# Six tiles in turn for the gathered rows of the routed experts, and each gather issued behind the turn that frees its tile

## The chip, the cores and the metric

The kernel runs on one core of a Trainium2 chip. The metric is the device time of one execution in microseconds; for the kernel before it is 903.7 us, the median of 3 runs from 902.4 to 906.5. Inputs and outputs lie in the chip's DRAM, tiles that engines work on lie in SBUF, and matrix products are written to PSUM.

## The reference, cut to what matters

Three layers follow each other, all in float32:

```python
# 1. delta-rule attention, 4 x 8 heads, 768 tokens, head_dim 48  -> x [3072, 384]
# 2. routed mixture: 8 experts, each token goes to the one with the largest logit
logits = x @ w_gate
e_idx  = np.argmax(logits, axis=1)
for e in range(8):
    mask = e_idx == e
    h  = np.maximum(x[mask] @ w1[e], 0.0)          # 384 -> 1024
    ye = h @ w2[e]                                 # 1024 -> 384
    out[mask] = gate_w[mask, None] * eom[mask, e, None] * ye
# 3. a dense mixture over all 3072 rows
h = np.maximum(np.maximum(x @ w1, x @ w2), x @ w3) # 384 -> 768, float64 weights
y = (h @ w_out)                                    # 768 -> 384
```

What counts here is layer 2: the rows of one expert lie scattered over x, so each expert's rows have to be gathered before they can be multiplied.

## The kernel before, in words

**Stages.** The attention with the routing of its rows fills about the first third of the time, the routed experts the second, the dense mixture the last. The order of the work on each engine is written out by hand: a unit (a small function) is given a time as a fraction of its run, the units of a run are sorted by that fraction, and each engine then executes its own instructions strictly in that order. A fraction therefore sets only the order; when an instruction starts is decided by its engine and by semaphores.

**Runs.** The routed experts are worked off in ten runs (`Moe.run`, line 1106). Runs 0 to 3 have 256 rows each, in two chunks of 128; runs 4 to 9 have 440, 416, 404, 388, 380 and 368 rows, in four chunks of 110, 104, 101, 97, 95 and 92 (`CAPS`, line 656). The weights of a run have a key: runs 4 to 9 have the keys 2 to 7.

**A run's steps.** `ids` (line 834) loads the entries of a run's list. `gather` (line 850) brings one chunk's rows, 1536 bytes each, from the DRAM tensor xd into a tile xg, with an indirect DMA that GpSimd (POOL) issues. `xpose` (line 863) turns a block of 128 features of all chunks of a run on TensorE, ScalarE makes the hi part and VectorE the lo part (xh, xl); a run has three such turns. `m1` (line 889) is the first product, eight units of nine matmuls, after which ScalarE and VectorE make hh and hl; `o1` (line 904) is the second product, three units of 24 matmuls, copied out by ScalarE into y.

**Where the turns lie.** In runs 2 to 8 the order on TensorE is: eight m1, turn 0 of the next run, o1 number 0, turn 1, o1 number 1, turn 2, o1 number 2. So turn 0 of run k + 1 stands between the two products of run k, and it needs all chunks of run k + 1.

**The gathers before the change.** There are four tiles xg, taken in turn over all chunks. The gathers of run 4 are issued, in POOL's order, at the start of run 3, and those of run k + 1 at the start of run k for k from 3 to 8 (line 1141); those of run 3 at the start of run 1, those of run 2 near the end of run 0 (line 1131).

**What else stands in the queues.** POOL also makes the lo part of the second weight of the next run, four instructions `w_..l` (`split`, line 700, and line 1145), placed from 0.5 of the run on, each behind ScalarE's hi part. The queue of SyncE (SP) loads the raw weights: the first weight (line 1147) at 0.6 and the second (line 1149) at 0.15 of a run, each into one tile that the split of the weight before must have read. It also moves 24 pieces of the dense mixture's weights (`Decode.units`, line 611), which VectorE and ScalarE work on between the units of the runs (line 1155), four pieces per run in runs 4 to 8.

**Memory.** The tiles xg are in the pool gp. The pool named moe (line 679) is opened after the attention's pools have been closed; the results y (line 910) lie in it, two tiles of 3 x 480 floats per partition.

Of the kernel before, what the change touches and what calls it, by code (L numbers as in the profile page):

```python
# [8 lines left out]
F32 = mybir.dt.float32  # L9
# [9 lines left out]
LIST = 3200          # entries of an expert's list  # L19
COLS = 3584          # of the first mixture's result  # L20


def merge(*lists):
    """Interleaves lists of units evenly."""
    items = []
    for li, l in enumerate(lists):
        n = len(l)
        for j, f in enumerate(l):
            items.append(((j + 0.5) / n, li, j, f))
    items.sort(key=lambda t: t[:3])  # L30
    return [t[3] for t in items]


class Attn:
    """Delta-rule attention in chunks of 32 tokens, and the routing of its rows.

    With k raw, n = |k| + 1e-6 and w = b / n^2 of a chunk's rows:
      U = (I + diag(w) tril(K K', -1))^-1 diag(w) (diag(n) V - K S)
      Y = Q S + tril(Q K', -1) U,  S <- S + K' U
    A sequence's eight heads are (j, b), j of 2, b of 4; g is the sequence: pairs (j = 0, 1) for each b, g.  # L40
    Partitions of the tiles of k, v and u: (b, 32 tokens); of y: (g, 32 tokens). "h" below is (g, j).
    """

    def __init__(s, ctx, tc, psum, big, hp, gp, kqt, knv, bt, wgt, xd, tab, ctab, cum, ident, wrm, x2):
# [4 lines left out]
        s.NI = 24          # chunks  # L49
        s.NP = 12          # pairs of chunks  # L50
        s.NSL = 6          # slabs of four chunks
# [7 lines left out]
        s.NA = 24          # units of stage A before the chain  # L59
# [6 lines left out]
        # slabs; steps of the chain: for the loads and scales, start and end of the inverses  # L66
        # of the vector engine, microseconds for the inverses in the steps of the chain
# [14 lines left out]
    def consts(s):  # L82
# [6 lines left out]
        # -beta of the blocks' tokens: partition (chunk of the slab, h, b), free (slab, k)  # L89
# [11 lines left out]
        # lists without tokens; an entry: row of xd, factor, token  # L101
# [9 lines left out]
        # routing  # L111
# [29 lines left out]
    # ---- stage A: the products of a chunk's tokens  # L141
    def loadKQ(s, i):
        """K' | Q' of a chunk: partition (head of a pair, d), free (b, pair of heads, k | q, t)"""
# [48 lines left out]
    # ---- stage B: inverses of four chunks; partition (chunk, h, b), free (i, k)  # L192
# [6 lines left out]
    def inv_n1(s, sl):  # L199
        """|k|^2 from the diagonals, then the strict triangles alone"""  # L200
# [7 lines left out]
    def inv_n2(s, sl):  # L208
        """n^2 = |k|^2 + 2e-6 |k| + 1e-12"""
# [12 lines left out]
    def inv_n3(s, sl):  # L222
        """-w, and n with one step of Newton for 1 / |k|"""
# [13 lines left out]
    def inv_step(s, ms):  # L237
        """Step m of one slab, in two parts, or of two slabs, [(slab, m)]: each hides the other's latency"""
# [37 lines left out]
    def steps(s, starts):  # L276
        """[(slabs that begin, time, unit, slabs that end)] of the inverses of slabs, {slab: first index}"""
# [12 lines left out]
    # ---- stage C: the chain over the chunks  # L290
    def load32(s, i):
        """Rows of k and v: partition (b, t), free (h, d)"""
        if i >= s.NI:
            return
        s.kv[i] = s.p2.tile([128, 2, 8, 48], F32, tag="kv", name=f"kv{i}", bufs=3)
        s.nc.sync.dma_start(s.kv[i], s.knv[i])
# [92 lines left out]
    # ---- stage R: routing of four chunks' rows  # L389
# [10 lines left out]
    def r_l(s, q):  # L400
        """The two gates' products of four chunks' rows: partition (chunk, gate and expert)"""
# [71 lines left out]
    def r_s(s, us):  # L473
        """A routing's rows go into the lists."""
# [5 lines left out]
    def warm(s, n):  # L480
        """Keeps the tensor engine's clock up over a wait."""
# [6 lines left out]
    # ---- the schedule  # L488
    def run(s, pre, tail):
# [15 lines left out]
        # the scales of slabs 1 and 2 as well  # L505
# [18 lines left out]
        # units of the inverses and of stage A over the steps; step -1 is before the chain  # L524
# [68 lines left out]
class Decode:  # L593
    """float64 weights, given as their 64 bits, to float32r parts: w = hi + lo, in DRAM.

    hi has a weight's sign, exponent and first 11 bits after the point; lo the rest, rounded to 12 bits.
    Weights under float32's normal range become 0.
    """

    N = 384          # doubles of a piece, per partition  # L600
# [10 lines left out]
    def units(s, raw, w):  # L611
        """Units of the next piece; raw: a function that gives its [128, 2 N] int32; w: [128, 4 N] int32"""
# [23 lines left out]
class Run:  # L636
    """A part of an expert's list: n entries in chunks of ct, its weights' key, the tags of their tiles."""
# [7 lines left out]
class Moe:  # L645
    """Both mixtures over rows that the routing has put into lists, one list per expert.

    Experts 0 and 1 come in two parts each: the first has tokens of the first 16 chunks, while the
    routing goes on. The others come in the order of their counts. The results follow each other
    without gaps as columns of x2, their tokens and factors in ctab.  # L650
    Float32 products: each operand is split exactly into two float32r parts, hi + lo; a product is
    hi hi + hi lo + lo hi.
    """
# [4 lines left out]
    def __init__(s, tc, cp, big, hp, gp, xd, x2, tab, ctab, w1, w2, dec, out):  # L658
# [5 lines left out]
        s.nh = 0  # L664
        nc, G = s.nc, s.nc.gpsimd
        # row: counts, limits, 8 zeros, starts, experts 2 to 7 of the runs, first parts' counts, experts 0 and 1, excess
# [14 lines left out]
    # ---- weights  # L681
# [585 lines left out]
```

## Time and profile before

| | |
|---|---|
| time, median of 3 runs (range) | 903.7 us (902.4 to 906.5) |
| span of the profiled execution, first to last instruction | 901.6 us |
| mean granted TensorE clock, share of full | 0.958 |
| TensorE matmul busy | 793.7 us, 88% of the span |
| VectorE busy | 478.3 us, 53% |
| ScalarE busy | 318.0 us, 35% |
| GpSimd busy | 251.0 us, 28% |
| gathers of routed rows | 32 |

The profiled execution has no time of its own beside its span; the span is 2.1 us under the median of the runs. PE is TensorE, DVE is VectorE, ACT is ScalarE, POOL is GpSimd, SP is SyncE, and SPq is SyncE's instruction queue, which issues DMAs. L868 is line 868 of the kernel. A timeline row reads: start and duration in us, engine, line, operation, output tile <- input tiles, shape, count, and in brackets how long the engine had been idle before and what ended that. A busy share is an average over stages with different limits, so it is read stage by stage.

### The profile page before, as it was taken

To read this page: it belongs to the slowest core of one execution; us is meant where nothing else is said; L and a number is where in the kernel's file an instruction comes from. 1 tells how busy PE (TensorE), PEld (TensorE's weight loads), DVE (VectorE), ACT (ScalarE), POOL (GpSimd) and SP (SyncE) were. 2 spreads that over 40 slices of the span, in tenths; PEclk is the share of its full clock that TensorE was granted. 3 is DMA by queue.
4 is the path that set the end of the run, shared out by engine and by line. 5 is a ranking of instruction groups with operands and counts; after the bars stand their busy time and mean duration, and the time that the engine had idled before them with its cause. 6 is when DMAs were issued, how large, how long until landed. Compare 5 with 4: busy or idle time off the path is not lost. (4 is left out here: it accounts for less than half of the span.)

```text
span 901.6 us, 20554 instructions
## 1 busy us (share of the span) xinstructions
PE 793.7 (88%) x8555; PEld 646.4 (72%) x8557; DVE 478.3 (53%) x1168; ACT 318.0 (35%) x733; POOL 251.0 (28%) x332
## 2 busy tenths in 40 slices
PE   9999877777777988997585898999999999999996
PEld 4544545445555987987574897978989898888886
DVE  2547899999465624979292966523232322323130
ACT  1112567667666313544141443221212222212221
POOL 2303455864344230436161342100101000010101
PEclk9999999989999998999696998999999999999999
DMA  8696465465953245577373757580202010000001
GB/s 226 189 228 152 91 175 168 127 173 150 287 132 102 72 136 194 181 251 221 118 214 122 230 196 275 175 332 0 71 1 62 10 54 17 9 27 1 36 0 37
DMA packets 99948, 118.18 MB, mean 131 GB/s; under 512 B 66516, under 2 KB 79771, under 8 KB 97163
## 3 DMA queue, kind: packets, MB, share of 16 engines
q1 hardware_dynamic: 62747, 92.42, 33.2%
q0 software_dynamic: 10384, 15.14, 5.6%
q10 hardware_dynamic: 26720, 9.26, 4.7%
q8 instruction: 69, 1.13, 0.6%
q14 instruction: 28, 0.23, 0.1%
HBM read 81.12 MB, written 35.67 MB: 130 GB/s over the span
## 5 line engine op out<-in xcount | busy, mean ns | idle before, releaser
L880 PE MATMUL pm<-xhm,wm 128*128 128x512 f32 x648 | 204.8, 396 | 1.7 <-DMA wm<-wd 1.7
L949 DVE TENSOR_TENSOR work<-work,pm 128x512 f32<-128x512 f32 x72 | 49.6, 689 | 186.7 <-PE pm L880 186.7
L880 PEld LDWEIGHTS pm<-xhm,wm 128*128 128x128 f32 x648 | 121.7, 188 | 31.1 <-DMA wm<-wd 2.2
L880 PE MATMUL pm<-xlm,wm 128*128 128x512 f32 x324 | 128.1, 396 | 0.0
L962 POOL DMA_INDIRECT out_dram<-work,idm x24 | 23.5, 981 | 304.0 <-ACT work L961 278.1
L249 DVE TENSOR_TENSOR zt<-Z 128x108 f32<-128x108 f32 (+36 forms) x254 | 79.7, 354 | 1.2
L351 ACT COPY Ubd<-pU 32x192 f32<-32x192 f32 x192 | 59.6, 310 | 56.0 <-PE pU L343 52.0
L951 ACT CAST hmh<-work 128x512 fp32r<-128x512 f32 x36 | 22.4, 621 | 156.2 <-DVE work L949 156.2
L880 PE MATMUL pz<-wm,hmh 128*128 128x384 f32 x288 | 73.1, 334 | 0.0
L255 DVE TENSOR_TENSOR Z<-Z,zt 128x108 f32<-128x108 f32 (+36 forms) x254 | 72.7, 326 | 0.1
L880 PEld LDWEIGHTS pm<-xlm,wm 128*128 128x128 f32 x324 | 60.9, 188 | 14.4
L363 PE MATMUL pS<-Ubd,kv 128*48 128x192 f32 x368 | 44.4, 375 | 21.8 <-ACT Ubd L351 18.2
L169 PEld LDWEIGHTS pg<-KQT 48*32 48x32 f32 x1536 | 36.7, 156 | 33.2 <-issue 31.0
L853 POOL DMA_INDIRECT xg<-xd,ids x32 | 48.2, 1507 | 40.3 <-PE pt L868 26.3
L868 PE MATMUL pt<-ident,xg 128*128 128x128 f32 (+6 forms) x96 | 19.0, 285 | 45.5 <-DMA xg<-xd,ids 45.5
L169 PE MATMUL pg<-KQT 48*32 48x64 f32 x1536 | 54.5, 311 | 0.6 <-issue 0.3
L872 DVE TENSOR_TENSOR xl<-pt,xh 128x256 fp32r<-128x256 f32 (+6 forms) x27 | 14.0, 523 | 76.9 <-ACT xh L871 76.9
L880 PEld LDWEIGHTS pz<-wm,hmh 128*128 128x128 f32 x288 | 52.1, 188 | 0.5
L363 PEld LDWEIGHTS pS<-Ubd,kv 128*48 128x48 f32 x368 | 22.5, 136 | 41.1 <-ACT Ubd L351 32.7
L486 PE MATMUL pwarm<-wrm 128*128 128x512 bf16 x82 | 48.4, 611 | 1.6 <-DVE wrm L1183 1.6
L868 PEld LDWEIGHTS pt<-ident,xg 128*128 128x128 f32 (+6 forms) x96 | 12.2, 147 | 50.8 <-DMA xg<-xd,ids 34.7
L880 PE MATMUL pz<-wm,hml 128*128 128x384 f32 x144 | 48.1, 334 | 0.0
(293 smaller groups left out, 1692.7 us busy)
## 6 DMA issues: line engine op xcount, KB each, us to landing
raw<-in_w_dram SPq DMA_DIRECT2D x13, 1536.0 KB
kv<-in_knv_dram SPq DMA_DIRECT2D x24, 384.0 KB
wd<-work SPq DMA_DIRECT2D x24, 384.0 KB
wm<-wd SPq DMA_DIRECT2D x8, 1152.0 KB
KQT<-in_kqt_dram ACTq DMA_DIRECT2D x13, 448.0 KB
KQT<-in_kqt_dram SPq DMA_DIRECT2D x11, 448.0 KB
xd<-x SPq DMA_DIRECT2D x24, 192.0 KB
x<-zero POOLq DMA_DIRECT2D x12, 384.0 KB, 4.7
```

The costliest lines, as they stand in the source:

```text
L169: nc.tensor.matmul(ps[b * 32:b * 32 + 32, o:o + 64], kq[:, 0, :], kq.rearrange("p k t -> p (k t)"), start=True, stop=True, tile_position=( ...
L249: nc.vector.tensor_mul(t, Z[:, a:e, m].unsqueeze(2).to_broadcast([128, e - a, n]), Z[:, m, m + 1:].unsqueeze(1).to_broadcast([128, e - a, n]))
L255: nc.vector.tensor_add(Z[:, a:e, m + 1:], Z[:, a:e, m + 1:], t)
L351: nc.scalar.copy(dst, src)
L363: nc.tensor.matmul(s.pS[q][j * 64:j * 64 + 48, g2 * 192:g2 * 192 + 192], s.kv[i][:, 0, h, :], s.Ubd[h // 4][:, h % 4, :], start=(i == 0 an ...
L486: s.nc.tensor.matmul(ps[:, 0:512], s.ones, s.wrm, start=True, stop=True)
L853: s.nc.gpsimd.indirect_dma_start(t[0:r.ct], None, s.xd[0:2049] if k < 2 else s.xd, bass.IndirectOffsetOnAxis(s.gid[k][0:r.ct, c, 0:1], 0))
L868: nc.tensor.transpose(ps[:, j * r.ct:j * r.ct + r.ct], s.xg[k][j][0:r.ct, c * 128:c * 128 + 128], s.ident[0:r.ct, 0:r.ct])
L880: s.nc.tensor.matmul(ps, a, b, start=(start and k == 0), stop=(stop and k == n - 1))
L949: nc.vector.tensor_max(m, m, ps)
L951: nc.scalar.copy(hi, m)
L962: nc.gpsimd.indirect_dma_start(s.out, bass.IndirectOffsetOnAxis(i[:, c, 2:3], 0), y, None, bounds_check=3071, oob_is_err=False)
```

## The change

The chunks of all runs are numbered through, 0 to 31, in a list `rowsets`. Chunk n takes tile n mod 6: four of the six are the old tiles xg, two are new tiles xr in the pool moe, while the two tiles y there shrink from 480 to 440 columns. The gathers of runs 0 to 2 stay where they were. From chunk 6 on, each gather has the place right behind the turn (of the same run's loop) that has read its tile's former chunk for the last time: in run 1 at 0.0 for the tiles of runs 0 and 1 and at 0.845 for those of run 2, in the later runs at 0.665, behind turn 2 at 0.66. The loads of the lists move from 0 to -0.01 of run 1.

So the loop of run 1 issues the two chunks of run 3 and the four of run 4, run 2 issues the chunks 0 and 1 of run 5, run 3 the chunks 2 and 3 of run 5 and 0 and 1 of run 6, run 4 the rest of run 6 and 0 and 1 of run 7, run 5 the rest of run 7 and 0 and 1 of run 8, run 6 the rest of run 8 and 0 and 1 of run 9, and run 7 the rest of run 9. In POOL's order those of runs 3 to 7 stand between the second and the third of the four `w_..l` instructions. The diff also drops comments and docstrings.

```diff
+        s.rowsets = [(k, c) for k, r in enumerate(s.runs) for c in range(r.ch)]
...
     def gather(s, k, c):
         r = s.runs[k]
-        t = s.gp.tile([128, 384], F32, tag="xg", name=f"xg{k}_{c}", bufs=4)
+        n = s.rowsets.index((k, c)) % 6
+        pool, tag, bufs = (s.gp, "xg", 4) if n < 4 else (s.p, "xr", 2)
+        t = pool.tile([128, 384], F32, tag=tag, name=f"xg{k}_{c}", bufs=bufs)
...
-            s.y[k] = s.p.tile([128, 3, 480], F32, tag="y", name=f"y{k}", bufs=2)
+            s.y[k] = s.p.tile([128, 3, 440], F32, tag="y", name=f"y{k}", bufs=2)
...
-                us += [(0, lambda: [s.ids(j) for j in range(4, 10)]), (0.0, lambda: rows(3))]
-            if 3 <= k < last:
-                us += [(0, lambda: rows(k + 1))]
+                us += [(-0.01, lambda: [s.ids(j) for j in range(4, 10)])]
+            if k:
+
+                free = [j for j in range(len(s.rowsets) - 6) if max(s.rowsets[j][0] - 1, 1) == k]
+                for j in free:
+                    t = 0.0 if s.rowsets[j][0] < 2 else 0.845 if k == 1 else 0.665
+                    us += [(t, lambda n=s.rowsets[j + 6]: s.gather(*n))]
```

## Rows read from the trace of the kernel before

**Rows 1.** Waits, longest first: engine, line, what for; us, times, longest.

```profile
PE pt L868 <- DMA xg<-xd,ids: 45.5, 19, 6.8
```

**Rows 2.** Timeline of TensorE: the turns of run 6's rows, in run 5.

```profile
429.63 0.40 PE L868 MATMUL pt<-ident,xg 101*128 101x101 f32 x1 [6.05 <-DMA xg<-xd,ids]
438.81 0.43 PE L868 MATMUL pt<-ident,xg 101*128 101x101 f32 x1 [5.48 <-DMA xg<-xd,ids]
...
445.68 0.51 PE L868 MATMUL pt<-ident,xg 101*128 101x101 f32 x4
...
450.58 0.51 PE L868 MATMUL pt<-ident,xg 101*128 101x101 f32 x4
```

**Rows 3.** Timeline of TensorE: turns 0 and 1 in runs 4, 6, 7 and 8.

```profile
391.62 0.25 PE L868 MATMUL pt<-ident,xg 104*128 104x104 f32 x1
...
399.29 0.52 PE L868 MATMUL pt<-ident,xg 104*128 104x104 f32 x4
...
475.86 0.39 PE L868 MATMUL pt<-ident,xg 97*128 97x97 f32 x1 [6.78 <-DMA xg<-xd,ids]
...
491.01 0.50 PE L868 MATMUL pt<-ident,xg 97*128 97x97 f32 x4
...
513.49 0.25 PE L868 MATMUL pt<-ident,xg 95*128 95x95 f32 x1
...
523.96 0.49 PE L868 MATMUL pt<-ident,xg 95*128 95x95 f32 x4
...
546.01 0.24 PE L868 MATMUL pt<-ident,xg 92*128 92x92 f32 x1
...
557.52 0.48 PE L868 MATMUL pt<-ident,xg 92*128 92x92 f32 x4
```

**Rows 4.** Stages: window, us; busy us of PE, PEld, DVE, ACT, POOL; clock, DMA share, GB/s.

```profile
401.50:408.50 7.00, 7.00 (x39) 6.55 (x38) 5.69 (x6) 2.12 (x4) 3.55 (x2) 1.00 0.12 18
409.60:423.40 13.80, 13.75 (x74) 13.22 (x72) 13.52 (x20) 8.37 (x14) 11.13 (x5) 1.00 0.86 271
423.40:438.90 15.50, 1.53 (x5) 0.65 (x5) 6.03 (x12) 0.52 (x1) 1.69 (x1) 0.60 0.74 224
438.90:443.30 4.40, 4.40 (x14) 4.20 (x15) 0.58 (x1) 1.68 (x3) 1.82 (x1) 0.50 0.02 6
443.30:456.40 13.10, 13.10 (x75) 12.93 (x74) 8.34 (x12) 4.46 (x9) 3.80 (x2) 0.99 0.11 31
```

**Rows 5.** Timeline of POOL around the start of run 5.

```profile
411.18 2.13 POOL L714 TENSOR_TENSOR w_3l<-raw,w_3h 128x768 fp32r<-128x768 f32 x1 [2.79 <-ACT w_3h L713]
413.49 2.22 POOL L853 DMA_INDIRECT xg<-xd,ids  x1 [0.18 <-issue]
416.02 3.06 POOL L853 DMA_INDIRECT xg<-xd,ids  x1 [0.30 <-issue]
```

**Rows 6.** Gathers by tile, issue to landing: runs 7 and 8.

```profile
DMA to landing us min/median/max: 16.4/16.9/18.8
...
DMA to landing us min/median/max: 5.4/9.3/9.8
```

**Rows 7.** DMA queue of POOL: packets, MB, share, while run 6's rows are gathered.

```profile
q0 software_dynamic: 2240, 0.65, 11.4%
```

**Rows 8.** Timeline of VectorE in run 5.

```profile
411.52 2.01 DVE L632 TENSOR_SCALAR work<-work 128x384 int32<-128x384 int32 x1
...
428.09 0.58 DVE L901 SCALAR_TENSOR_TENSOR hl<-ph,hh 128x416 fp32r<-128x416 f32 x1
428.59 0.35 DVE L632 TENSOR_SCALAR work<-work 128x384 int32<-128x384 int32 x1
```

**Rows 9.** Timeline of SP's queue in run 5, then run 7's load and its first reader.

```profile
414.96 0.41 SPq L697 DMA_DIRECT2D raw<-in_w_dram  x1
...
506.07 0.38 SPq L697 DMA_DIRECT2D raw<-in_w_dram  x1
...
518.72 0.84 ACT L713 CAST w_6h<-raw 128x768 fp32r<-128x768 f32 x1
```

## Prediction

> **What bounds the kernel now.** I read the engines' shares first: TensorE's matmuls are busy for 88% of the span, no other engine for more than 53%, so in most stages the end is set by TensorE's own order, and what can be won are the stretches in which it stands still. The list of waits, read next, has one large entry that belongs to the routed experts: TensorE's turns wait 45.5 us, in 19 waits, for gathered rows [rows 1]. The timeline of TensorE shows where. In run 5 the first product is done at 429.63 - 6.05 = 423.58 us, and the four transposes of turn 0 then come one by one as their chunks land, the last at 438.81 [rows 2]. Runs 4, 6, 7 and 8 have the same pattern, shorter or as long [rows 3]. The stage view shows what it costs beyond the wait: in the gap TensorE is busy 1.53 of 15.5 us, and in the 4.4 us behind it the granted clock is 0.50, that is 1.2 of 2.4 GHz, and only then full again [rows 4]. Since the engine is in order and everything behind the routed experts hangs on it, a us of this gap is a us of the whole.
>
> Why the rows are late is seen on POOL: run 6's gathers begin at 413.49, behind the last of the four splits of the second weight (411.18 + 2.13), one after the other at 2.2 to 3.1 us each [rows 5], and the last of them is turned at 438.81. Run 7's, under the same conditions, land 16.4 to 18.8 us after issue; run 8's, with 95 rows, in 5.4 to 9.8 us [rows 6]. The time from the start of a run to its turn 0 is only 13.8 us [rows 4].
>
> **What goes.** For each run I take the time from the end of the first product (or the start of turn 0 where the first chunk was there) to turn 1, and compare it with an undisturbed stretch of one turn and one o1 unit. That is turn 1 to turn 2 in run 5, 450.58 - 445.68 = 4.90 us at 416 columns [rows 2], scaled by columns for the others: 5.18 at 440, 4.76 at 404, 4.57 at 388, 4.48 at 380.
>
> Run 4: 399.29 - 391.62 = 7.67, minus 5.18: 2.5.
> Run 5: 445.68 - 423.58 = 22.10, minus 4.90: 17.2.
> Run 6: 491.01 - (475.86 - 6.78) = 21.93, minus 4.76: 17.2.
> Run 7: 523.96 - 513.49 = 10.47, minus 4.57: 5.9.
> Run 8: 557.52 - 546.01 = 11.51, minus 4.48: 7.0 [rows 2, 3].
>
> Sum 49.8 us; the part of it over the bare waits is the clock and the turns done piecemeal. The waits of turns before run 4, which the rest of the 45.5 us is, stay: those gathers keep their places or hang on lists that come no earlier.
>
> **Does the new order bring the rows in time?** The chunks 0 and 1 of a run are now issued more than one and a half runs ahead; chunks 2 and 3 come first in the group behind turn 2 of the run before the one that turns them, so they decide. All times in this part are shifted by what has been won before them. For run 6's chunk 3: turn 2 of run 4 ends near 402.5, the gather in front takes 2.2 to 3.1 us and 0.3 of gap, so chunk 3 starts near 405.5, and it is needed at 423.58 - 2.5 = 421.1. That leaves 15.6 us. At the landing times of run 8 nothing is left to wait; at the longest seen, 18.8, some 3.2 us are. The issue now falls into a stage where the DMA share was 0.12 (401.5 to 408.5), in place of 0.86 [rows 4], so I take no wait, and keep 3.2 us for each of runs 5 and 6 as the other end.
>
> The slow gathers are those of 101 and 97 rows, and run 6's four make 2240 packets of 0.65 MB, some 290 bytes each, where a row has 1536 [rows 7]. So part of the 16 us may be the gather's own and not the busy queue's. The Trainium skill, "DMA: Bandwidth & Descriptors", section "Why a DMA increments its semaphore by 16 and not by 1", says that a transfer is spread over the largest number of engines up to 16 that divides its slowest dimension, which for a prime count of rows is one. By that rule 16 us would stay in a quiet queue too, and run 5 would wait 0.4 us; the trace's slow gathers, the two prime counts, agree with it, though the number of packets is nothing that it explains.
>
> **What is added or moved.** No matmul, copy or byte is added; the 24 gathers from chunk 8 on are moved, each DMA with its instruction, all on POOL. Three things they move past.
>
> First, POOL's splits. The third and fourth split now stand behind the gathers. The group in run 4 is the largest, four gathers of 101 and 97 rows: 4 x (2.7 + 0.3) = 12 us from 402.5 (2.7 lies between the two durations shown), then two splits of 2.1 us, done near 418.7 [rows 5]; the run starts near 407.2. The second product that reads them starts at 421.4 and comes to the fourth part 3.4 us later. So it is hidden, with 6 us to spare; at 3.06 us each still 4.5. Runs 3 and 5 issue two long and two short gathers, some 9 us, runs 6 and 7 less.
>
> Second, SP's queue. The raw tile of the second weight is free when the fourth split has read it, so the load that stood at 414.96 (412.5 shifted) goes out near 418.8, and SP's queue stands still from 412.5. Behind it stand the loads and stores of the pieces of the dense mixture; the pieces due in the first product are loaded before it, and the next is worked on behind turn 0, so I take nothing for them, and at most the 6.3 us of the standstill once. The weight is first read by ScalarE right behind turn 0, near 422. In run 7 the load at 506.07 was read at 518.72 without a wait for it, so it takes at most 12.6 us [rows 9]; from below, 1.5 MB at the 271 GB/s of this stage are an estimate of 5.8 us. It lands between 424.6 and 431.4, and ScalarE waits 3 to 9 us. The cover is the o1 unit: y of unit 0 must be copied before unit 2 takes its PSUM bank, at 421.4 + 9.5 = 430.9. So TensorE loses nothing to some 1.5 us in this run, where the group is longest; I take nothing, nearest to the estimate, because the gathers no longer share the stage with that load.
>
> Third, VectorE. It was busy 13.52 of 13.80 us in the first product of run 5 and wrote the last hl at 428.67, 5.1 us behind TensorE [rows 4, 8]. Before, the gap covered that; now the second product reads it as its 23rd matmul, 0.3 + 7 x 0.575 + 0.2 = 4.5 us behind the end of the first product. So hl is late next, by 0.6 us in run 5 and about as much in run 6, nothing in the others, whose products come with fewer columns or, in run 4, with VectorE less far behind. A POOL split that runs beside it makes a 0.35 us operation take 2.01 [rows 8]; two splits per run move from the second product into the next first product, the gathers the other way. From turn 2 to the next turn 0, which is what the lag is summed over, it is the same work; I take 1 us over all runs, between nothing and the 13 us of the rival below.
>
> The wait that is added, of each gather for the turn in front of it, stalls only POOL: behind it are the two splits, whose hi parts ScalarE makes behind that turn as well. The loads of lists at -0.01 and the narrower y cost nothing: SP's order around them is the same, and y is used to 440 columns at most.
>
> **Sum.** 49.8 - 1.2 - 1.0 = 47.6 us. 901.6 - 47.6 = 854.0 of span, and with the 2.1 us by which the runs' median lies over the span 856 us, 5.3% less. By the bounds above alone: up to 853.9 with no loss at all, and, with 3.2 us twice, their clock, and 1.5 us for ScalarE, about 866.
>
> **Rivals.**
> *VectorE becomes the bound.* Over run 5 it was busy 13.52 + 6.03 + 0.58 + 8.34 = 28.5 us [rows 4], and a run without the gap lasts some 28.5. If the two moved splits cost 2.01 - 0.35 = 1.65 us each in a stage with no idle time and nothing comes back in the second product, that is 3.3 us in each of four runs, 13 in all: 869. For it: 13.52 of 13.80. Against it: 8.34 of 13.1 us in the second product, where it has room for what the first pushes on.
> *The prime gathers still come late.* Run 5 and 6 wait 1 to 4 us each and the clock falls behind the wait, as it did for some 2 us in run 5 (22.1 us against 15.2 of gap and 4.9): up to 11 us, so 857 to 867, 862 as a middle. For it: the 16.9 us of run 7. Against it: 15.6 us of lead.
> *Slower: the second weight comes late and holds ScalarE, and through it TensorE.* Place: the load behind POOL's fourth split, in runs 4 to 7. From the point at which it lands 9.8 us behind the first product, each us more is one of TensorE. If it takes the longest the trace allows for run 5 (issued at 414.96, first read only behind the last chunk's transpose at 438.81), 24 us, it lands near 443, 12 us too late; four such runs give 48 and the dropping clock behind each 8 more: 912. Against it: the 12.6 us of run 7.
> *The change doesn't do what it says:* the two new tiles lie in memory of the closed pools and their first gathers, run 2's, wait for old readers; then only a few us change at run 2's turn and the rest still comes: 860.
>
> **How the numbers follow.** The forecast has 0.70 (853 to 862), VectorE 0.12, late prime gathers 0.10, old readers 0.03, slower 0.03, and 0.02 is left for a gain of a few us that ends within half a per cent, such as gathers stuck early. From 851 (a little under the sum without any loss, for the spread of the runs) to 870 holds the first three with some to spare for each. Half a per cent, 4.5 us, is about what a measurement of this kernel can tell: faster 0.95, same 0.02, slower 0.03.
>
> **What would show it.** Right: the wait of TensorE's turns for gathered rows falls from 45.5 to under 10 us, all of it before run 4; no stage at clock 0.50 behind turn 0 in runs 5 and 6; a run 5 of some 29 us; gathers between the second and third split. The term of VectorE: idle time of TensorE in the second product put down to hl, about 0.6 us in runs 5 and 6. Wrong: that wait in many runs (VectorE), turns of 101 and 97 rows still waiting (prime gathers), ScalarE waiting for raw over 9 us with TensorE idle at o1's third unit (second weight).

## The result, and the profile after

The changed kernel takes 864.8 us (median of 4 runs, 861.3 to 868.5) beside 905.1 us (902.4 to 913.5) for the kernel before on the same chip: a ratio of 0.954, 95% interval 0.950 to 0.959. A second set of runs gave 863.8 beside 902.3 us, 0.958 (0.953 to 0.963). The forecast was 856 us with a range of 851 to 870. The range holds the time. The likeliest case's own span, 853 to 862, does not: of the 47.6 us that were forecast some 40 came.

The profiled execution has a span of 862.1 us in place of 901.6. Ahead of the routed stage executions differ, whatever the kernel (run 1 begins between 305 and 312 us in these traces), so below I compare the routed stage alone, from run 1's first matmul to the dense mixture's first. It lasts 281.1 us before (309.50 to 590.63) and 241.9 after (310.18 to 552.05), 39.2 less.

The list of waits of the kernel after (line numbers of the new kernel: turns L872, products L884, the low halves `hl` L905, splits L715 and L716, gathers L857) answers to [rows 1]:

```profile
PE pt L872 <- DMA xg<-xd,ids: 8.7, 4, 4.0
...
PEld ph L884 <- DVE hl L905: 8.4, 11, 1.7
...
PE ph L884 <- DVE hl L905: 4.7, 8, 1.3
...
PE po L884 <- DVE hl L905: 2.4, 2, 1.3
```

The 45.5 us have become 8.7, in four waits, all before run 4. What is new is the second thing to see: TensorE waits for VectorE's `hl` in both products. The timeline of TensorE at the turns of run 6's rows answers to [rows 2]: four transposes in half a us, each time, without a wait.

```profile
425.95 0.51 PE L872 MATMUL pt<-ident,xg 101*128 101x101 f32 x4
...
430.86 0.51 PE L872 MATMUL pt<-ident,xg 101*128 101x101 f32 x4
...
435.76 0.51 PE L872 MATMUL pt<-ident,xg 101*128 101x101 f32 x4
```

The stage view (columns as in [rows 4]) of run 5's first product, its turn 0 and first unit of the second product, and the same two stages of run 6: the clock is 1.00 throughout, that is 2.4 GHz, where before it was 0.60 in the gap and 0.50 behind it [rows 4], and VectorE is busy 14.04 of 15.90 and 14.19 of 15.10 us.

```profile
410.10:426.00 15.90, 14.05 (x74) 13.29 (x73) 14.04 (x19) 8.47 (x14) 9.95 (x5) 1.00 0.79 224
426.00:430.90 4.90, 4.90 (x30) 4.76 (x29) 4.80 (x11) 1.74 (x3) 0.00 (x0) 1.00 0.70 263
440.60:455.70 15.10, 14.00 (x77) 13.27 (x76) 14.19 (x20) 8.29 (x14) 6.85 (x5) 1.00 0.91 289
455.70:460.50 4.80, 4.80 (x30) 4.60 (x29) 4.73 (x10) 2.28 (x4) 1.53 (x1) 1.00 0.33 111
```

TensorE's timeline, product by product, says where the rest of the gain went. First products of runs 4 to 8, before: 14.58, 13.92, 13.59, 13.11, 13.02 us (68.2 in all); after: 15.71, 16.00, 15.02, 14.35, 13.81 (74.9), so 6.7 more. The first unit of the second product, whose undisturbed size is that of the third unit of the same run, 23.3 us over the five runs, takes 26.4, 3.1 more, nearly all of it in runs 7 and 8 (5.89 and 5.93 us where the third units take 4.48 and 4.35). Run 2's first product has 1.0 more. The 49.8 us that the turns were to give, less 6.7, 3.1 and 1.0, make 39.0; measured 39.2.

A second profile of the same kernel (experiment 4) has the same long first products, but run 6's first unit takes 6.23 us in place of 4.73 and run 7's 6.34: these two sums come to 11.7 us there, where they are 9.7 here (6.7 and 3.1 before rounding).

What one of the long first products looks like from inside: four engines in run 5's, first VectorE, then POOL, ScalarE and TensorE.

```profile
413.92 2.96 DVE L716 TENSOR_TENSOR w_4l<-raw,w_4h 128x1024 fp32r<-128x1024 f32 x1 [0.46 <-ACT w_4h L715]
416.80 0.58 DVE L905 SCALAR_TENSOR_TENSOR hl<-ph,hh 128x416 fp32r<-128x416 f32 x1
418.20 0.80 DVE L628 SCALAR_TENSOR_TENSOR work<-work 128x384 int32<-128x384 int32 x1 [0.82 <-DMA wd<-work]
419.03 2.08 DVE L629 SCALAR_TENSOR_TENSOR work<-work 128x384 fp32r<-128x384 f32 x1
421.03 0.58 DVE L905 SCALAR_TENSOR_TENSOR hl<-ph,hh 128x416 fp32r<-128x416 f32 x1
...
413.59 2.14 POOL L857 DMA_INDIRECT xg<-xd,ids  x1 [0.31 <-issue]
415.75 4.93 POOL L716 TENSOR_TENSOR w_3l<-raw,w_3h 128x768 fp32r<-128x768 f32 x2
...
422.61 0.56 ACT L626 ACTIVATE work<-work 128x384 f32<-128x384 f32 x1 [2.45 <-DMA work<-in_mb_dram]
423.07 1.10 ACT L904 ACTIVATE hh<-ph 128x416 fp32r<-128x416 f32 x2
...
421.66 0.46 PE L884 MATMUL ph<-xh,w_3h 128*128 128x416 f32 x1 [1.31 <-DVE hl L905]
424.16 0.46 PE L884 MATMUL ph<-xh,w_3h 128*128 128x416 f32 x1 [0.54 <-DVE hl L905]
```

POOL's third and fourth split run at 415.75 to 420.68, behind the gathers. VectorE's low part of the first weight, 1.21 us elsewhere, takes 2.96 beside the last gather and the first of these splits; then VectorE stands 0.82 us for a piece's store; then its L629, 0.56 us elsewhere, takes 2.08 beside the last split. The `hl` queued behind all this comes at 421.03; TensorE, which needs it to go on, has waited 1.31 us. The second wait hangs on ScalarE: it stands 2.45 us for a piece's load (issued by SP at 412.50, ready some 10 us later), so two `hh` and the next `hl` are late.

### The profile page after: what moved, and what is told of

Same layout as the page of the kernel before. It is cut to its first block, busy times and chain, and to the rows that moved or that the text cites. A ratio compares the mean times of both kernels' runs of the same rounds, so it can differ in the third digit from the quotient of the medians.

```text
span 862.1 us, 20554 instructions
## 1 busy us (share of the span) xinstructions
PE 785.1 (91%) x8556; PEld 637.2 (74%) x8557; DVE 483.1 (56%) x1168; ACT 319.1 (37%) x733; POOL 250.2 (29%) x332
## 5 line engine op out<-in xcount | busy, mean ns | idle before, releaser
L884 PE MATMUL pm<-xhm,wm 128*128 128x512 f32 x648 | 204.8, 396 | 0.8 <-DMA wm<-wd 0.8
L884 PEld LDWEIGHTS pm<-xhm,wm 128*128 128x128 f32 x648 | 121.7, 188 | 30.2 <-DMA wm<-wd 1.2
L884 PE MATMUL pm<-xlm,wm 128*128 128x512 f32 x324 | 128.1, 395 | 0.0
L249 DVE TENSOR_TENSOR zt<-Z 128x108 f32<-128x108 f32 (+36 forms) x254 | 81.7, 361 | 1.2
L955 ACT CAST hmh<-work 128x512 fp32r<-128x512 f32 x36 | 22.4, 622 | 155.2 <-DVE work L953 155.2
L884 PE MATMUL pz<-wm,hmh 128*128 128x384 f32 x288 | 73.1, 334 | 0.0
L884 PEld LDWEIGHTS pm<-xlm,wm 128*128 128x128 f32 x324 | 60.9, 188 | 14.4
L255 DVE TENSOR_TENSOR Z<-Z,zt 128x108 f32<-128x108 f32 (+36 forms) x254 | 70.9, 319 | 0.1
L363 PE MATMUL pS<-Ubd,kv 128*48 128x192 f32 x368 | 47.7, 400 | 19.7 <-ACT Ubd L351 19.5
L857 POOL DMA_INDIRECT xg<-xd,ids x32 | 44.5, 1392 | 45.2 <-PE pt L872 30.6
L884 PEld LDWEIGHTS pz<-wm,hmh 128*128 128x128 f32 x288 | 52.1, 188 | 0.5
L884 PE MATMUL pz<-wm,hml 128*128 128x384 f32 x144 | 48.1, 334 | 0.0
L370 ACT COPY Sbd<-pS 48x384 f32<-48x384 f32 x92 | 43.5, 473 | 6.2 <-PE pS L363 4.7
L477 POOL DMA_INDIRECT tab<-rdat,rpos x24 | 30.8, 1282 | 41.5 <-DMA tab<-rdat,rpos 32.7
L915 ACT COPY y<-po 128x256 f32<-128x256 f32 (+6 forms) x30 | 13.3, 444 | 72.4 <-PE po L884 72.4
```

What stands on the lines that cost most here:

```text
L249: nc.vector.tensor_mul(t, Z[:, a:e, m].unsqueeze(2).to_broadcast([128, e - a, n]), Z[:, m, m + 1:].unsqueeze(1).to_broadcast([128, e - a, n]))
L255: nc.vector.tensor_add(Z[:, a:e, m + 1:], Z[:, a:e, m + 1:], t)
L363: nc.tensor.matmul(s.pS[q][j * 64:j * 64 + 48, g2 * 192:g2 * 192 + 192], s.kv[i][:, 0, h, :], s.Ubd[h // 4][:, h % 4, :], start=(i == 0 an ...
L370: nc.scalar.copy(dst, src)
L477: s.nc.gpsimd.indirect_dma_start(s.tab, bass.IndirectOffsetOnAxis(pos[:, u:u + 1], 0), dat[:, u, :], None)
L857: s.nc.gpsimd.indirect_dma_start(t[0:r.ct], None, s.xd[0:2049] if k < 2 else s.xd, bass.IndirectOffsetOnAxis(s.gid[k][0:r.ct, c, 0:1], 0))
```

## Experiments

Twelve runs follow; 4 and 11 repeat a kernel. "Long" below is the sum of two things over runs 4 to 8, from TensorE's timeline: first products over the 68.2 us of the kernel before, and first units of the second product over the undisturbed 23.3.

**1. Six tiles, the gathers at their old places.**

```diff
-            if k:
...
-                for j in free:
...
-                    us += [(t, lambda n=s.rowsets[j + 6]: s.gather(*n))]
+            if k == 1:
+                us += [(0.0, lambda: rows(3))]
+            if 3 <= k < last:
+                us += [(0, lambda: rows(k + 1))]
```

> The changed kernel's six tiles, with every gather at its old place (those of run k + 1 at the start of run k, on GpSimd behind the fourth split). Theory (the place in GpSimd's order makes the rows late, the number of tiles alone frees nothing): 900 to 908 us, turns of runs 4 to 8 wait some 38 us as before. Rival (the gathers were held by their tiles): near 865 us, waits gone.

Measured 900.6 beside 900.9 us, ratio 1.002 (0.998 to 1.006). The waits of turns are the old ones:

```profile
PE pt L872 <- DMA xg<-xd,ids: 43.5, 19, 6.9
```

The two tiles buy nothing by themselves. As long as a run's gathers are issued at that run's predecessor's start, they have no use for more room.

**2. Four tiles, each gather issued behind turn 2.**

```diff
-        n = s.rowsets.index((k, c)) % 6
-        pool, tag, bufs = (s.gp, "xg", 4) if n < 4 else (s.p, "xr", 2)
+        pool, tag, bufs = s.gp, "xg", 4
...
-                    us += [(t, lambda n=s.rowsets[j + 6]: s.gather(*n))]
+                    us += [(t, lambda n=s.rowsets[j + 4]: s.gather(*n))]
```

> The old four tiles, each gather issued behind the turn that frees its tile, so all four chunks of run k + 1 go out behind turn 2 of run k - 1. Theory (issue time decides; six tiles only give chunks 0 and 1 a head start): the last chunk of 101 rows is issued some 12 us behind turn 2, lands 16 to 18 us later, 5 to 8 us too late, the same for 97 rows; the others land in time: 872 to 880 us. Rival (the head start of about a run is needed for all): 890 or more. Rival (six tiles buy nothing): 863 to 868.

Measured 876.6 us, ratio 0.971 (0.966 to 0.976), routed stage 257.4 us. TensorE's waits at the turns of run 6's rows (line L871 in this kernel):

```profile
PE pt L871 <- DMA xg<-xd,ids: 18.6, 7, 4.9
...
422.28 0.34 PE L871 MATMUL pt<-ident,xg 101*128 101x101 f32 x2
425.53 0.31 PE L871 MATMUL pt<-ident,xg 101*128 101x101 f32 x1 [2.92 <-DMA xg<-xd,ids]
429.29 0.43 PE L871 MATMUL pt<-ident,xg 101*128 101x101 f32 x1 [3.46 <-DMA xg<-xd,ids]
```

The earlier place takes 24 of the 39 us. The two tiles, which bring half of a run's gathers a whole run earlier, take the other 15.5: with four, chunks 2 and 3 of run 6 still come 2.9 and 3.5 us late.

**3. The kernel before, without prime row counts.** Runs 6 and 7 gather their rows in four chunks of 101 and of 97. Four more places each make it 102 and 98; nothing else is touched.

```diff
-    CAPS = (440, 416, 404, 388, 380, 368)
+    CAPS = (440, 416, 408, 392, 380, 368)
```

> The kernel before with 408 and 392 rows for runs 6 and 7's lists in place of 404 and 388, so chunks of 102 and 98 rows in place of 101 and 97. Theory (a gather of a prime count of rows is slow by itself): the packets of run 6's gathers fall from 2240 to some hundreds, their landing from 16 to 9 us, the waits at the turns of these two runs from 14.0 and 14.9 us to about 4 each with little of the clock's fall: some 22 to 26 us less, 878 to 883 us. Rival (DMA load of those runs makes them late): 903 to 906 us, landing still 16 us.

Measured 866.8 us, ratio 0.958 (0.953 to 0.963): more than any theory had given it, and by time not to be told from the changed kernel, in the old order with the old four tiles. Its profiled execution is the longest of its four; there the routed stage is 251.1 us, 30.0 less than before, where the changed kernel has 39.2 less. The DMA queue of POOL while run 6's rows are gathered, their landing, and the waits of turns in all:

```profile
q0 software_dynamic: 448, 0.63, 12.3%
...
DMA to landing us min/median/max: 4.9/8.1/8.9
...
PE pt L868 <- DMA xg<-xd,ids: 21.0, 15, 3.6
```

448 packets in place of 2240 for as many bytes [rows 7], and 4.9 to 8.9 us to landing (run 7's 98 rows: 4.5 to 9.9), where run 7's 97 rows took 16.4 to 18.8 [rows 6]. The gathers stand where they stood, and the stage is as full as before: a mean DMA share of 0.94 from 401.5 to 416 us, where the kernel before has 0.80 from 413.5 to 439. So it was mostly the row count that made the rows late, not the stage's other traffic; the turns of runs 5 to 8 still wait some 3 to 4 us each. Another effect lies where I had not looked: the lists of the same rows go through SP. Its queue in the kernel before, then in this one:

```profile
321.42 9.62 SPq L839 DMA_DIRECT2D ids<-tab  x6
331.22 0.64 SPq L697 DMA_DIRECT2D raw<-in_w_dram  x1
```

```profile
317.39 3.68 SPq L839 DMA_DIRECT2D ids<-tab  x6
321.26 1.78 SPq L697 DMA_DIRECT2D raw<-in_w_dram  x1
```

Six loads of lists, two of them with a prime number of partitions, hold the queue 9.62 us before and 3.68 here; the weight's load behind them goes out 6 us sooner against the lists. Run 2's first product takes 11.14 us here in place of 16.25, but that this follows from the shorter queue is not shown: in all six profiles with these row counts the lists hold the queue 3.6 to 3.9 us, and run 2's first product takes 11.14 and 11.41 us in experiments 3 and 6, but 15.8 to 16.8 in 7, 10, 11 and 12. What holds for the gathers alone is the stage from run 3's first matmul on: 233.0 us before, 210.6 here, 192.6 in the changed kernel (194.6 in experiment 4). That is 22.4 of 40.4 us.

**4. The changed kernel again**, unedited, beside the others:

> The changed kernel once more, as the measure for the three that follow: 862 to 868 us; every theory expects the same.

863.8 us, routed stage 242.6 us; long by 11.7, as said above.

**5. POOL's last two splits ahead of the gathers.**

```diff
-                us += spread(s.split(k - 1, 0, A, V), 0.05, 0.35) + spread(s.split(k - 1, 1, A, G), 0.5, 1)
+                us += spread(s.split(k - 1, 0, A, V), 0.05, 0.35) + spread(s.split(k - 1, 1, A, G), 0.5, 0.66)
```

> The changed kernel with the four splits of the second weight placed from 0.5 to 0.66 of a run in place of 0.5 to 1, so that all four stand ahead of the gathers on GpSimd and none runs beside the next first product. Theory (two splits back to back behind the gathers hold VectorE for up to 4.8 us in a stage where it has no idle time, which is most of the 9 to 10 us that the forecast missed): the first products of runs 4 to 8 shorten by 5 us or more in all, 856 to 861 us. Rival (VectorE is short of time whatever the order): within 2 us of the changed kernel. Rival (three splits in a row now hold xl, which the next run needs): slower than it, 866 or more.

Measured 862.5 us, ratio 0.956 (0.951 to 0.960): not to be told from the changed kernel. The edit moves ScalarE's hi parts of that weight as well. Run 4's first product is back at 14.58 us, as it is in experiment 6 without this edit, so either edit frees it; but runs 5 and 6 have 15.46 and 16.60, and the gathers, now later, are waited for again in run 5:

```profile
415.48 0.46 PE L884 MATMUL ph<-xh,w_3h 128*128 128x416 f32 x1 [0.76 <-DVE hl L905]
417.97 0.46 PE L884 MATMUL ph<-xh,w_3h 128*128 128x416 f32 x1 [0.54 <-DVE hl L905]
421.31 0.30 PE L872 MATMUL pt<-ident,xg 101*128 101x101 f32 x1 [1.12 <-DMA xg<-xd,ids]
```

**6. The changed kernel without prime counts** (the edit of 3).

> The changed kernel with 408 and 392 rows in place of 404 and 388 (chunks of 102 and 98 rows). Theory (the groups of slow gathers on GpSimd push the splits and through them the second weight's load): the group in run 4 falls from some 10 to 6 us, ScalarE's wait for raw in run 5 (2.95 us) goes, the first product of run 5 loses part of its 2 us: 2 to 4 us less than the changed kernel, 861 us. Rival (only VectorE counts): same as the changed kernel, or 0.5 us more for the added columns.

Measured 854.8 us, ratio 0.949 (0.944 to 0.954), routed stage 234.2 us, 7.7 less than the changed kernel's. 5.9 of these are run 2's first product (11.41 us for 17.27), which experiment 7, with the same row counts, doesn't repeat (16.13). Runs 4 to 8 are hardly shorter: long by 8.9 in place of 9.7.

**7. Both: splits ahead, no prime counts.**

> Both of the edits: splits ahead of the gathers and chunks of 102 and 98 rows. If the two losses are separate, their gains add: 854 to 859 us. If both act through VectorE in the first product, it is no better than splits ahead alone.

Measured 851.7 us, ratio 0.944 (0.939 to 0.949), routed stage 234.0 us; long by 5.9. First products of runs 4 to 6 are now 14.57, 13.60 and 13.60 us, no longer than before the change. In runs 7 and 8 they stay at 13.90 and 14.59, with first units of 6.33 and 6.32. So there were two causes: what lengthened runs 4 to 6 went with the place of POOL's splits and the prime gathers together, in 7 and 8 it was another.

**8. Less work for VectorE.** The last two of the seven operations that VectorE does on each of 24 pieces of the dense mixture's weights are left out (those weights' low parts are not made).

```diff
-            lambda: V.tensor_scalar(c, hi, -0x800000, None, ALU.bitwise_and),
-            lambda: V.scalar_tensor_tensor(r(k), k, 2.0 ** -34, f(c), ALU.mult, ALU.mult)], store
```

> The changed kernel, with the last two VectorE operations of each of the 24 pieces of the dense mixture's weights left out (the mask and the last multiply, 0.35 + 0.56 us a piece beside nothing else; those weights' low parts are then not computed). Theory: the 9.9 us by which the first products of runs 4 to 8 and the first second products of runs 7 and 8 are longer than in the kernel before are VectorE's shortage. With 0.9 us less for each of the four pieces of a run most of it goes: first products of 13.6 us, the waits of the first products for the hidden rows' low half (8 of 1.3 us in the changed kernel) nearly all gone, a routed stage of some 233 to 236 us and 855 to 858 us in all. Rival: the shortage is on SP's queue, where a second weight's load waits behind a piece and its store; then nothing but the VectorE row changes, and the time stays at 862 to 866.

Measured 870.8 us, ratio 0.962 (0.957 to 0.966), routed stage 251.9: 10 us longer with less work (by time 6 to 7, and there the intervals of the two ratios overlap). Neither theory had this. First products are shorter (70.3 in all for 74.9), but the first units of runs 4 to 6 take 9.66, 9.85 and 8.22 us. VectorE's waits show why:

```profile
DVE work L628 <- DMA wd<-work: 16.4, 6, 4.1
```

```profile
394.24 2.07 DVE L628 SCALAR_TENSOR_TENSOR work<-work 128x384 int32<-128x384 int32 x1 [4.09 <-DMA wd<-work]
396.23 0.60 DVE L903 SCALAR_TENSOR_TENSOR hl<-ph,hh 128x440 fp32r<-128x440 f32 x1
```

A piece's operations are spread evenly over a run, and the third of them writes a buffer that the store of the piece before last must have left. Two operations fewer bring it nearer to that store in VectorE's order; it stalls for the store, and the `hl` behind it is what the second product then waits for. The edit had changed the order as well as the work, so it decided nothing.

**9. The same, with the order kept**: the two operations stay in their places and work on 16 of 384 columns.

```diff
-            lambda: V.tensor_scalar(c, hi, -0x800000, None, ALU.bitwise_and),
-            lambda: V.scalar_tensor_tensor(r(k), k, 2.0 ** -34, f(c), ALU.mult, ALU.mult)], store
+            lambda: V.tensor_scalar(c[:, 0:16], hi[:, 0:16], -0x800000, None, ALU.bitwise_and),
+            lambda: V.scalar_tensor_tensor(r(k[:, 0:16]), k[:, 0:16], 2.0 ** -34, f(c[:, 0:16]), ALU.mult, ALU.mult)], store
```

> The changed kernel, with the last two VectorE operations of each of the 24 weight pieces kept in their places in the order but done on 16 of 384 columns (so most of those weights' low parts are not computed). Leaving them out altogether had brought the piece's next operation nearer to the store that it waits for (4.1 us where the changed kernel waits 0.8), and six such stalls of VectorE held the second products; here the order has as many places as before. Theory: VectorE's shortage is what lengthens the first products of runs 4 to 8 and the first second products of runs 7 and 8 by 9.9 us; some 0.7 us less work a piece, 2.8 us a run, takes 5 to 9 us of it: a routed stage of 233 to 237 us in place of 242, 856 to 860 us in all. Rival: what holds VectorE is the wait for a piece's store, which comes up sooner as soon as VectorE is quicker: waits for the store of over 8 us in all, and no gain, 862 us or more.

Measured 856.5 us, ratio 0.949 (0.946 to 0.952). The time lies in the theory's range, but it came by another way than the theory said: the routed stage lost 3.5 us (238.4), not 5 to 9, and the rest lies outside it, where executions differ anyway. The waits for the store were 0.6 us, so the rival falls. By runs it is plain. Runs 7 and 8 have first products of 13.11 and 12.97 us, those of the kernel before; there VectorE's amount of work was the cause. Their first units, 5.40 and 5.80 us, are still 2.4 of 3.0 us too long and still wait for `hl`, so the work taken away answers for about half of what these two runs had lost. Runs 4 to 6 have 15.72, 15.68 and 14.98, as if nothing had been taken away, because there one stretched operation is enough:

```profile
416.37 2.08 DVE L629 SCALAR_TENSOR_TENSOR work<-work 128x384 fp32r<-128x384 f32 x1
418.37 0.58 DVE L905 SCALAR_TENSOR_TENSOR hl<-ph,hh 128x416 fp32r<-128x416 f32 x1
...
419.00 0.46 PE L884 MATMUL ph<-xh,w_3h 128*128 128x416 f32 x1 [0.98 <-DVE hl L905]
```

**10. Two of the pieces moved into the last run**, on top of 7.

```diff
-    NP = {2: 2, 3: 2, 4: 4, 5: 4, 6: 4, 7: 4, 8: 4}
+    NP = {2: 2, 3: 2, 4: 4, 5: 4, 6: 4, 7: 3, 8: 3, 9: 2}
...
+            if k == last:
+                us += spread(pieces.pop(0) + pieces.pop(0), 0.03, 0.5)
```

> The kernel with six tiles, no prime counts and the low half of the second weight's POOL split ahead of the gathers, and of the 24 pieces of the dense mixture's weights one less in each of runs 7 and 8 and two in run 9, which had none. Theory: VectorE is short in runs 7 and 8, where the first of the second products came to 6.3 us in place of 4.5, and has time in run 9: 2 to 4 us less than with the pieces as they were, 847 to 850. Rival: run 9's first product then waits for VectorE in turn, or the last pieces' stores delay the dense mixture's first load of weights: no gain, 851 to 855.

Measured 855.3 us, ratio 0.945 (0.940 to 0.949); kernel 7, run again beside it, 854.1. No gain, but both theories were right in their places. Runs 7 and 8 got back most of what experiment 7 had left: 13.58 and 12.63 us, first units 5.76 and 4.36, together 5.4 us less than in kernel 7 beside it. The last run lost more: its second product took 19.76 us in place of 12.16. SP's queue, then ScalarE:

```profile
525.04 0.40 SPq L620 DMA_DIRECT2D work<-in_mo_dram  x1
525.53 15.83 SPq L623 DMA_DIRECT2D wd<-work  x3
...
535.82 0.55 ACT L626 ACTIVATE work<-work 128x384 f32<-128x384 f32 x1 [9.33 <-DMA work<-in_mo_dram]
536.27 1.20 ACT L904 ACTIVATE hh<-ph 128x368 fp32r<-128x368 f32 x3
```

The second piece's load is issued behind the dense mixture's first weights and lands 10 us later; three `hh` stand behind the operation that waits for it.

**11. Kernel 7 again**, beside 8 and 10.

> The same kernel as splits_ahead_no_prime_counts, once more beside the two others: 849 to 855 us, and a routed stage of 234 us.

854.1 us, ratio 0.943 (0.940 to 0.947). Its routed stage was 237.6, beyond the 234 expected; it is long by 7.1, with 0.7 of it in run 5's first unit, which had nothing in experiment 7. Products of run 8 differ by up to 1.6 us between its two profiles (its second unit 4.37 and 5.93), so a single product of one profile is to be trusted no further than that.

**12. One piece in the last run** in place of two.

```diff
-    NP = {2: 2, 3: 2, 4: 4, 5: 4, 6: 4, 7: 3, 8: 3, 9: 2}
+    NP = {2: 2, 3: 2, 4: 4, 5: 4, 6: 4, 7: 4, 8: 3, 9: 1}
...
-                us += spread(pieces.pop(0) + pieces.pop(0), 0.03, 0.5)
+                us += spread(pieces.pop(0), 0.03, 0.45)
```

> The kernel with two pieces in the last run, with one piece in place of two there (run 7 has its four again, run 8 three). The second of the two had its load issued only at 525.04 us, behind the dense mixture's first weights, and landed near 535.7: ScalarE stood 9.33 us for it, and the last run's second product took 19.76 us in place of 12.16. With one piece its load goes out in run 8, some 11 us earlier. Theory: the last run is back at 12.3 us for either product, run 8's gain (its first product 12.6 us in place of 15.3, its first second product 4.4 in place of 6.3) stays: 849 to 852, 2 to 4 us less than the kernel without the move. Rival: the piece's load is late in the last run in any case: 853 to 857.

Measured 851.4 us, ratio 0.943 (0.939 to 0.946). The profiled execution is the longest of its six, so I read only its order: the last run's products are back at 12.32 and 12.16 us, so the load is no longer late; run 8's, 14.49 and 5.19 us where the theory had 12.6 and 4.4, do not show that its gain stayed. The time can't be told from kernel 7's. Kernels 7, 10 and 12 have the lowest ratios, 0.943 to 0.945, all faster than the changed kernel and the one before; between them nothing is decided.

## Why the prediction was right, and where its size was off

**The gain came as worked out.** The turns of runs 4 to 8 gave up the full 49.8 us: each takes half a us, no stage behind them runs at half the clock, and the waits that stay, 8.7 us, are those before run 4, as the prediction said.

**The rows are in time through their lead.** Run 6's chunks 0 and 1, issued in the window 379 to 384, took 13.8 to 17.3 us to land, at a mean DMA share of 0.65 and 0.66 from issue to landing; in the same group the 104-row gathers, issued before them, took 3.3.

```profile
DMA to landing us min/median/max: 13.8/15.6/17.3
...
DMA to landing us min/median/max: 3.3/3.3/3.3
```

The chunks that decide, 2 and 3, did not find the quiet stage that the prediction counted on either: the share was 0.75 and 0.73 where it had 0.12, and they took 13.0 and 13.7 us. Chunk 3, issued at 407.99, landed 4.2 us before turn 0, and half of that is luck: run 5's first product was 2.1 us longer.

A queue somewhat less full than the 0.80 before did not quicken them. The rule of the Trainium skill ("DMA: Bandwidth & Descriptors", section "Why a DMA increments its semaphore by 16 and not by 1"), by which the 16 us would stay, agrees with these numbers. The prediction had weighed it only for whether the lead would do, and left open how much of the 16 us was the gathers' own. Experiment 3 answers: 102 and 98 rows took 4.5 to 9.9 us at the same place, so some half of it, and with it 22 of the 40 us from run 3 on. So the change was right about the waits and worked around their cause. Where the cause is gone, the change still gives 251.1 - 234.2 = 16.9 us of the routed stage, 12.0 by the medians of two sets of runs. The prediction's "some 290 bytes each" took a mean for a size; the last section has the sizes.

**The second weight.** Its load went out at 420.71, as POOL's fourth split ended (forecast: near 418.8); ScalarE waited 2.95 us for it (forecast: 3 to 9), `y` was copied at 431.46, and run 5's units take 4.78, 4.78 and 4.77 us. Hidden, as said.

```profile
420.71 0.35 SPq L699 DMA_DIRECT2D raw<-in_w_dram  x1
...
430.00 0.83 ACT L715 CAST w_4h<-raw 128x768 fp32r<-128x768 f32 x1 [2.95 <-DMA raw<-in_w_dram]
```

**VectorE's term failed in its size.** It stood in the sum with 1.2 us for the late `hl` and 1.0 us for POOL's splits; measured are 9.7 in one profile and 11.7 in another, most of what the rival priced at 13. So the time fell between the forecast and that rival. The step that failed is the sentence that from turn 2 to the next turn 0 "it is the same work": the lag of VectorE is not summed over such a stretch but has to be held inside the first product, where TensorE stops at every `hl` that is too late. Two splits moved from the second product, where VectorE has idle time, into the first, where holds of VectorE like the 2.08 us one above cost TensorE up to 1.3 us at a time (the rows above and experiment 9). And a lag of VectorE at a first product's end, 5.1 us in run 5 before, fell into the gap of turn 0; with the gaps gone runs 7 and 8 pay for its work (experiments 9 and 10; in 9 for about half of what they lost). I had priced the lag at the end of the product and not in its middle, and I had the rival's argument, 13.52 of 13.80 us, in front of me.

What stays open: how the 4.7 us by which runs 4 to 6 are long (6.3 in experiment 4) divide between POOL's splits and the piece's late load, and what else makes the first units of runs 7 and 8 late. With the splits moved alone runs 4 to 6 stayed at 4.7, without prime counts alone 3.3 were left, with both none, or 0.7 in the second profile (experiments 5, 6, 7 and 11). Also open is when run 2's first product takes 11 us and when 16.

## What to carry to other kernels

Before giving slow gathers more lead, ask why they are slow: look at the packets and the time to landing of a gather by its row count, and try a count with divisors. When a gap is closed, look for the engine whose lag the gap was paying for, and check it at each point where the next engine needs it, not as a sum over the stage. An experiment that takes work away from an engine moves all that stands behind it: keep the places in the order, and shrink what stands in them.

## What the runs showed of the hardware

A gather of 101 rows by POOL makes some 560 packets, one of 102 rows 112 (2240 and 448 for four). The mean of 290 bytes [rows 7] is no packet's size. The DMA view counts the small ones, with all queues together, first in the kernel before around run 5's gap, then without prime counts while run 6's rows are gathered:

```profile
DMA packets 4482, 7.24 MB, mean 205 GB/s; under 512 B 2297, under 2 KB 3705, under 8 KB 4225
...
DMA packets 2509, 6.78 MB, mean 271 GB/s; under 512 B 480, under 2 KB 1632, under 8 KB 2288
```

In the packets of the trace themselves, 1980 of POOL's 2240 have 12 bytes and 132 have 4608, which is three rows; of the 448, 200 and 120. Yet the packets' own time is the same, 49.3 us for either four gathers, so the many small packets take no engine time that would explain the late rows. A quarter of that, 12.3 us, is an estimate of what one gather would take if a single DMA engine did all of it; it lies just under the 13.0 to 19.3 us that 101 rows took to land in these traces. No view here shows the engines one by one.

The instruction on POOL is shorter too, beside the landing: 1.1 to 2.1 us where the 101 rows took 2.2 to 3.1 [rows 5]. In the kernel without prime counts:

```profile
401.52 1.11 POOL L853 DMA_INDIRECT xg<-xd,ids  x1 [0.17 <-issue]
402.93 2.10 POOL L853 DMA_INDIRECT xg<-xd,ids  x1 [0.30 <-PE ph L880]
405.34 1.26 POOL L853 DMA_INDIRECT xg<-xd,ids  x1 [0.30 <-issue]
```

A VectorE operation whose operands all lie in SBUF and that starts within a POOL split ends a fixed time behind it, wherever in the split it starts: 0.2 us behind for one that takes 0.35 alone, 0.4 for 0.56, 1.1 for 1.21. That holds for 36 of 37 in the kernel before and the changed one. Beside two splits in a row it can be held for both. In run 7 of the changed kernel, an operation that takes 0.56 us alone:

```profile
471.12 4.84 DVE L633 SCALAR_TENSOR_TENSOR work<-work 128x384 fp32r<-128x384 int32 x1
475.89 0.55 DVE L905 SCALAR_TENSOR_TENSOR hl<-ph,hh 128x388 fp32r<-128x388 f32 x1
...
471.89 3.65 POOL L716 TENSOR_TENSOR w_5l<-raw,w_5h 128x768 fp32r<-128x768 f32 x2
```

POOL's two splits end at 475.54, VectorE's operation at 475.96. It can also come between two: one that starts at 384.00 in run 4, within a split, ends at 386.87, and the next split, from 385.75, takes 2.82 us in place of 1.84. The operations with an operand in PSUM, as `hl` (0.53 to 0.62 us in all 48 of the changed kernel, where L633 goes from 0.54 to 4.84), were never stretched, though five of the 48 ran wholly beside a split; they are late only through what is queued in front of them. The Trainium skill, "SBUF — State Buffer", section "SBUF: two separate sides", has a pair of ports that VectorE and GpSimd share as an exclusive lock, held for a whole instruction. The trace agrees: held and not slowed in proportion. The page gives it to the one that starts first, and most rows bear that out (operations that start before a split, with no other work of POOL beside them, keep their length). The 4.84 us row does not: it starts at 471.12, within a gather of POOL (470.37 to 471.87) but before both splits, and comes behind both.
